# Seven products in place of eight for pairs of token blocks, in a retention and feed-forward kernel on one core

## The chip, the core and the metric

The program runs on one core of a Trainium2 chip. The metric is the time of one execution on the device in microseconds (us); lower is better. The engines have names of their own: PE (TensorE) multiplies matrices into PSUM, ACT (ScalarE) and DVE (VectorE) do elementwise work, POOL (GpSimd) does elementwise work on SBUF, and SP (SyncE) issues nearly all DMA transfers. Each engine takes its instructions strictly in the order of the program.

## The reference

```
scores = q @ k.T / sqrt(64)                      # 8 batches, 8 heads, 576 positions, head size 64
D[h,i,j] = gamma_h ** (i - j) if i >= j else 0   # gamma_h = 1 - 2**(-5-h)
x = (scores * D) @ v                             # 4608 tokens x 512
h = x @ w_in                                     # 512 -> 2048: the first product
out = (h - tanh(h)) @ w_out                      # 2048 -> 512: the second product
```

All arrays are float32.

## The kernel before

The 576 positions are cut into NC = 9 blocks of C = 64. A block holds 64 positions of all 8 batches, so BLK = 512 tokens. Per block three things are done.

*Retention* (`entry`, `entry3`; the matmuls have L287): for each batch and head 64x64 matmuls give the scores within the block (`s`), the new state (`new`) and the output (`own`, `two`), which adds the running `state` of the earlier blocks. The output x is written as two fp32r words, `xh` (rounded) and `xl` (the rest). From the third block on, a block's retention is three calls of `entry3` that lie in the FFN work of the block before. Its q, k and v are loaded by SP (`qk`, `vr`, `one`) and scaled by tables on POOL (`prep`, L237).

*First product* (`mm1`, L430): for each of NF = 16 slices f of the 2048 hidden columns, 12 matmuls of 128x128 weights by 512 tokens gather h(n, f) in one PSUM bank: 4 slices of the 512 inputs, times the three terms w_high·x_high, w_high·x_low, w_low·x_high. The bank is one of two (tag `h`).

*Second product* (`mm2`, L495): ACT makes tanh (L455), DVE subtracts (L456), ACT rounds `gh` (L457), DVE makes the rest `gl` (L458); then 12 matmuls of 512 columns add this slice into the four banks `o0` to `o3`. After slice 15 the banks are copied to `ob` and stored.

The weights arrive as raw words and are turned into two fp32r words each (`win`, `wout`), which stay in SBUF from then on. While this goes on, blocks 0 and 1 only do their first product (`seq`); its results go to DRAM (`spill`) and come back later in the loop `late`, which does the second products of block 1 and then of block 0 (`fetch`, `resume`, `words`). Blocks 2 to 8 then alternate `mm1` of one slice with `mm2` of the slice before. `in_order` holds each engine to the order in which the code is written. Tiles share places by `tag`; `bufs` is how many of a tag exist, and a tile that takes a place waits until all readers of the last one there are done.

## Time and profile before

| | |
|---|---|
| median of 3 runs | 882.23 us (882.13 to 883.61) |
| span of the profiled execution, first to last instruction | 881.9 us |
| time of that execution beside the span | none is listed; the median is 0.3 us above the span |
| PE busy | 872.7 us |
| DVE, ACT, POOL busy | 367.3, 294.4, 69.4 us |
| DMA | 82.06 MB, mean 93 GB/s |

A row of groups names the line, the engine, the operation, output <- inputs with their shapes, the count, and then busy us, mean ns of one, and idle time before. Matmuls overlap in the pipeline, so a matmul's duration in a row is longer than its share of the time; the chain of waits gives start, length and count of stretches of them. "PEclk" is the share of TensorE's clock that was granted.

### The profile page before, as it was taken

The page shows a single profiled execution, that of the slowest core. Times are in us where ns is not written, and L with a number is a line of the kernel's source. Part 1 is how long each engine was busy: PE and PEld are TensorE (multiplying, and loading weights), DVE is VectorE, ACT ScalarE, POOL GpSimd, SP SyncE. Part 2 cuts the span into 40 slices and gives each one's busy share as a digit, 9 for nine tenths or more (in the row PEclk, how much of TensorE's full clock was granted, in tenths as well). Part 3 has the DMA queues.
Part 4 walks back from the last instruction along what each step waited for, and adds up shares of the span by engine and source line. Part 5 has one row for each costly group of instructions (what it writes and reads, how often), then busy time and mean ns, then how long its engine had stood idle before and what let it go on. Part 6 is the DMA issues. An engine that isn't in the chain of part 4 may idle for free.

```text
span 881.9 us, 17730 instructions
## 1 busy us (share of the span) xinstructions
PE 872.7 (99%) x7846; PEld 724.3 (82%) x7846; DVE 367.3 (42%) x571; ACT 294.4 (33%) x525; POOL 69.4 (8%) x73
## 2 busy tenths in 40 slices
PE   7999999999999999999999999999999999999997
PEld 6888888888888888888888888888888888888886
DVE  5989876554332333323332433233232332232222
ACT  4887754443222222222222222222222222222222
POOL 0001001011110001101110111001110111000000
PEclk9999999999999999999999999999999999999999
DMA  8966945552410121203220141112120321002001
GB/s 307 374 237 220 367 154 167 142 164 77 116 49 30 49 68 55 78 1 97 73 79 1 50 119 50 30 47 62 62 78 1 97 73 48 1 2 48 1 1 48
DMA packets 37628, 82.06 MB, mean 93 GB/s; under 512 B 4144, under 2 KB 5296, under 8 KB 37552
## 3 DMA queue, kind: packets, MB, share of 16 engines
q1 hardware_dynamic: 37024, 80.02, 28.5%
q8 instruction: 61, 1.00, 0.5%
q10 hardware_dynamic: 528, 0.92, 0.3%
q14 instruction: 15, 0.12, 0.0%
HBM read 63.62 MB, written 17.30 MB: 92 GB/s over the span
## 4 chain that ended last, share of the span: by engine, by line
PE 98%; DMA 1%; ACT 0%; DVE 0%; SPq 0%; issue 0%
PE o L495 45%; PE h L430 45%; PE new L287 2%; PE s L287 2%; PE own L287 2%; PE two L287 1%; DMA rwi<-in_w_in_dram 1%; DMA a<-in_first_dram 1%; PE new_first L287 0%; PE own_first L287 0%; SPq L555 0%; ACT mi L100 0%; ACT xh L313 0%; ACT mi L105 0%; PE s_first L287 0%
## 5 line engine op out<-in xcount | busy, mean ns | idle before, releaser
L430 PE MATMUL h<-xh,wi 128*128 128x512 f32 x1152 | 302.8, 391 | 0.5 <-ACT xh L313 0.5
L495 PE MATMUL o<-wo,gh 128*128 128x512 f32 x1144 | 289.8, 391 | 0.0
L430 PEld LDWEIGHTS h<-xh,wi 128*128 128x128 f32 x1152 | 216.3, 188 | 46.3 <-ACT xh L313 0.7
L495 PEld LDWEIGHTS o<-wo,gh 128*128 128x128 f32 x1144 | 213.1, 188 | 45.0
L456 DVE TENSOR_TENSOR g<-h,g 128x512 f32<-128x512 f32 x114 | 78.8, 691 | 341.5 <-ACT g L455 341.4
L455 ACT ACTIVATE g<-h 128x512 f32<-128x512 f32 x114 | 68.2, 598 | 363.6 <-PE h L430 362.8
L495 PE MATMUL o<-wo,gl 128*128 128x512 f32 x572 | 157.2, 389 | 0.0
L430 PE MATMUL h<-xl,wi 128*128 128x512 f32 x576 | 154.2, 389 | 0.0
L430 PEld LDWEIGHTS h<-xl,wi 128*128 128x128 f32 x576 | 108.1, 188 | 22.6
L495 PEld LDWEIGHTS o<-wo,gl 128*128 128x128 f32 x572 | 107.4, 188 | 22.3
L458 DVE TENSOR_TENSOR gl<-g,gh 128x512 fp32r<-128x512 f32 x113 | 81.0, 717 | 77.6 <-ACT gh L457 72.8
L457 ACT CAST gh<-g 128x512 fp32r<-128x512 f32 x113 | 70.1, 621 | 86.0 <-DVE g L456 86.0
L237 POOL TENSOR_TENSOR vr<-vr,vtab 128x512 f32<-128x512 f32 x21 | 22.4, 1068 | 611.0 <-DMA vr<-in_qkv_dram 525.3
L287 PE MATMUL own<-qk,state 64*64 64x64 f32 x736 | 45.2, 221 | 0.0
L287 PE MATMUL own<-qk,vr 64*64 64x64 f32 x736 | 44.1, 218 | 0.0
L287 PEld LDWEIGHTS own<-qk,vr 64*64 64x64 f32 x736 | 36.8, 135 | 0.0
L287 PEld LDWEIGHTS own<-qk,state 64*64 64x64 f32 x736 | 36.7, 134 | 0.0
L478 DVE TENSOR_TENSOR gl<-s,gh 128x512 fp32r<-128x512 f32 x30 | 23.1, 770 | 24.2 <-PE o L495 13.6
L237 POOL TENSOR_TENSOR qk<-qk,qtab 128x512 f32<-128x512 f32 x20 | 28.4, 1421 | 53.5 <-DMA qk<-in_qkv_dram 53.5
L477 ACT CAST gh<-s 128x512 fp32r<-128x512 f32 x30 | 18.6, 621 | 30.0 <-PE o L495 17.3
L287 PE MATMUL s<-qk 64*64 64x64 f32 x736 | 25.5, 219 | 0.0
L313 ACT CAST xh<-own 128x512 fp32r<-128x512 f32 x25 | 14.7, 586 | 29.9 <-PE own L287 29.9
(85 smaller groups left out, 568.6 us busy)
## 6 DMA issues: line engine op xcount, KB each, us to landing
qk<-in_qkv_dram SPq DMA_DIRECT2D x23, 512.0 KB, 5.9
vr<-in_qkv_dram SPq DMA_DIRECT2D x23, 512.0 KB, 4.5
rwi<-in_w_in_dram SPq DMA_DIRECT2D x16, 512.0 KB, 5.4
rwo<-in_w_out_dram SPq DMA_DIRECT2D x16, 512.0 KB, 5.2
out_dram<-ob SPq DMA_DIRECT2D x61, 128.0 KB, 2.4
s<-spill_dram SPq DMA_DIRECT2D x30, 256.0 KB, 2.7
one<-in_qkv_dram SPq DMA_DIRECT2D x14, 512.0 KB, 5.4
spill_dram<-g SPq DMA_DIRECT2D x20, 256.0 KB, 4.3
```

The lines of the kernel that those rows point to most:

```text
L237: nc.gpsimd.tensor_tensor(a, a, table, op=ALU.mult)
L287: nc.tensor.matmul(out_, w, x, start=start, stop=stop)
L313: nc.scalar.copy(xh, o)
L430: nc.tensor.matmul(hp, win[f][:, a, cc, :], x[:, cc, :], start=(k == 0), stop=(k == 3 * NCC - 1))
L455: nc.scalar.activation(g, h, AF.Tanh)
L456: nc.vector.tensor_tensor(g, h, g, op=ALU.subtract)
L457: nc.scalar.copy(gh, g)
L458: nc.vector.tensor_tensor(gl, g, gh.bitcast(F32), op=ALU.subtract)
L477: nc.scalar.copy(gh, g)
L478: nc.vector.tensor_tensor(gl, g, gh.bitcast(F32), op=ALU.subtract)
L495: nc.tensor.matmul(ops[n][t], g[:, t * P : (t + 1) * P], wout[f_][:, a, :], start=(f_ == first and k == 0), stop=(f_ == final and k == 2),)
```

## The change

For blocks 3 to 8, taken in pairs (3,4), (5,6), (7,8), the first product is done for two blocks and two slices f at once. Tokens (block a, block b), inputs (two halves) and hidden columns (slice 2j, slice 2j+1) form 2x2 matrices of blocks, and the Winograd form of Strassen's scheme makes their product from seven products instead of eight, each with half the inputs: 2 slices times 3 terms = 6 matmuls of 512 columns (`product`).

- *Variants of the weights.* For each of 8 pairs of slices seven 256x128 weight matrices are needed. Three are pieces of the weights themselves, which `raw_words` writes to DRAM (`wvar`) during the second half of `late`. Four are sums (`variants`: POOL makes `r1`, `r2`, half of `ta` and of `tb`, DVE the other halves; ACT rounds, DVE makes the rest into `ot`, SP stores). They are made while block 2 does its first product.
- *Block 2* now does its whole first product at once; h - tanh(h) goes to DRAM, and its second product follows as a stage of its own (`stage_b(2, 0)`).
- *Stage A* (`stage_a`) of a pair does seven products for each j, additions on DVE, and block a's second product (`mm2_pair`). Block b's h - tanh(h) goes to DRAM. The variants come back from DRAM in slots of four (`load_slot`, 1 MB).
- *Stage B* (`stage_b`) is block b's second product alone, and between its slices the retention of the next pair: eight calls of `attend`, two batches each, for block a and block b in turn. It also makes the seven sums of tokens (`put`): hi words on ACT, low words on DVE, `t1`, `t3` on DVE and `t2`, `t4` on POOL.
- The loads of q, k, v and their scaling on POOL now go by turns of two batches (`load_turn`, `prep_turn`).

The core of the diff (`split`, `mm2_pair`, the new tags and the removed code of blocks 2 to 8 in other places are left out):

```diff
+NV = 7
+NPAIR = NF // 2
+FIRST = 3
...
-        if n == 0 or n == 1 and f < NF - 2:
+        if n == 1 and f >= NF - 2:
+            activate(n, f, hp, g)
+        elif n < 2:
 
             nc.scalar.copy(g, hp)
             pace.append(tc.nc.cur_bb.bb.instructions[-1].name)
             nc.sync.dma_start(spill[n, f], g)
         else:
-            activate(n, f, hp, g)
-
...
+            nc.scalar.activation(g, hp, AF.Tanh)
+            nc.vector.tensor_tensor(g, hp, g, op=ALU.subtract)
+            nc.sync.dma_start(spill[n, f], g)
...
+    def raw_words(f):
+
+        j, w = f // 2, win[f].bitcast(F32)
+        for v, cc in ((0, 0), (5, 2)) if f % 2 == 0 else ((6, 2),):
+            nc.sync.dma_start(wvar[:, NV * j + v].rearrange("p (s m) -> p s m", s=2), w[:, :, cc : cc + 2].rearrange("p s c m -> p s (c m)"))
+
...
+    turns = [(c + u) * B + b for c in range(FIRST, NC, 2) for b in range(0, B, 2) for u in range(2)]
+    work = pool.tile([P, 4, DM], F32, tag="xl1", bufs=1, name="work")
...
+    def load_turn(m, t):
+        if m >= len(turns):
+            return
+        j = turns[m]
+        c, b = divmod(j, B)
+        if t == 0 and (m == 1 or m % 8 == 0):
+            load_tables(c - m % 2)
+        if t == 0 and m % 3 == 2:
+            part = const.tile([P, 2, 2, 4, C], F32, tag=place_of(0), name=f"qk{j}")
+        elif t == 0:
+            part = pool.tile([P, 2, 2, 4, C], F32, tag="qk", bufs=2, name=f"qk{j}")
+        else:
+            part = pool.tile([P, 2, 2, 4, C], F32, tag=("vr", "one")[m % 2], bufs=1, name=f"vr{j}")
+        nc.sync.dma_start(part, qkv_d[c - 1, b : b + 2, :, 2 * t : 2 * t + 2].rearrange("u p t i s -> p u t i s"))
+        parts[j, t] = part
+        for u in range(2):
+            loaded.setdefault(j + u, Parts([None, None])).parts[t] = part[:, u]
...
+    def put(v, b, src, sub):
+
+        hi, lo = [x[:, :, b * C : (b + 2) * C].rearrange("p i (u t) -> p u i t", u=2) for x in xv[v]]
+        if sub == 0:
+            nc.scalar.copy(hi, src)
+        else:
+            nc.vector.tensor_tensor(lo, src, hi.bitcast(F32), op=ALU.subtract)
...
+    def attend(m, between):
+
+        j = turns[m]
+        c, b = divmod(j, B)
+        first, states = (c - FIRST) % 2 == 0, c < NC - 1
+        if first and b == 0:
+            new_xv()
+        o = bank(f"own{j}", "own")
+        outs, same = pair(m_out, j, o), []
+        if states:
+            new = bank(f"new{j}", "new")
+            same += pair(m_state, j, new)
+        more = m + 1 < len(turns)
+        if more:
+            sc = bank(f"s{turns[m + 1]}", "h")
+            same = pair(m_score, turns[m + 1], sc) + same
+        run(same, outs)
+        if more:
+            after_score(turns[m + 1], sc, 2)
+        if first:
+            a = pool.tile([P, 2, 4, C], F32, tag="cv", bufs=4, name=f"xa{j}")
+            kept[b] = a
+            put(0, b, o[:, :, 0:2], 0)
+            put(5, b, o[:, :, 2:4], 0)
+            nc.scalar.copy(a, o)
+            if states:
+                add_state(j, new)
+            between()
+            put(0, b, o[:, :, 0:2], 1)
+            put(5, b, o[:, :, 2:4], 1)
+        else:
+            a = kept.pop(b)
+            t13 = pool.tile([P, 2, 2, 2, C], F32, tag="cv", bufs=4, name=f"t13_{j}")
+            t24 = pool.tile([P, 2, 2, 2, C], F32, tag="cv", bufs=4, name=f"t24_{j}")
+            t1, t3, t2, t4 = t13[:, 0], t13[:, 1], t24[:, 0], t24[:, 1]
+            own = pool.tile([P, 2, 4, C], F32, tag="cv", bufs=4, name=f"xb{j}")
+            nc.scalar.copy(own, o)
+            put(4, b, o[:, :, 2:4], 0)
+            nc.vector.tensor_tensor(t3, own[:, :, 2:4], own[:, :, 0:2], op=ALU.subtract)
+            nc.gpsimd.tensor_tensor(t2, t3, a[:, :, 0:2], op=ALU.add)
+            nc.vector.tensor_tensor(t1, own[:, :, 0:2], a[:, :, 0:2], op=ALU.subtract)
+            nc.gpsimd.tensor_tensor(t4, a[:, :, 2:4], t2, op=ALU.subtract)
+            if states:
+                add_state(j, new)
+            put(3, b, t3, 0)
+            put(2, b, t1, 0)
+            between()
+            put(4, b, o[:, :, 2:4], 1)
+            put(3, b, t3, 1)
+            put(2, b, t1, 1)
+            put(1, b, t2, 0)
+            put(6, b, t4, 0)
+            put(1, b, t2, 1)
+            put(6, b, t4, 1)
+        prep_turn(m + 2, 0)
+        prep_turn(m + 1, 1)
+        load_turn(m + 3, 0)
+        load_turn(m + 2, 1)
...
+    def variants(j):
+
+        f1, f2 = [win[2 * j + u].bitcast(F32) for u in range(2)]
+        r1, r2, ta, tb = [pool.tile([P, 2, 2, P], F32, tag="cv", bufs=4, name=f"{n}{j}") for n in ("r1", "r2", "ta", "tb")]
+        if j == 0:
+            ots = [pool.tile([P, 2, 2, 2, P], F32R, tag="xh1", bufs=1, name=f"ot{j}_{u}") for u in range(2)]
+        else:
+            ots = [const.tile([P, 2, 2, 2, P], F32R, tag=place_of(2 * j - 2 + u), name=f"ot{j}_{u}") for u in range(2)]
+        for r, f in ((r1, f1), (r2, f2)):
+            nc.gpsimd.tensor_tensor(
+                r.rearrange("p k c m -> p (k c) m"), f[:, 0], f[:, 1], op=ALU.add,
+            )
+        nc.gpsimd.tensor_tensor(ta[:, 1], r2[:, 0], r2[:, 1], op=ALU.add)
+        nc.gpsimd.tensor_tensor(tb[:, 0], r1[:, 0], r2[:, 0], op=ALU.subtract)
+        nc.vector.tensor_tensor(ta[:, 0], ta[:, 1], r1[:, 0], op=ALU.subtract)
+        nc.vector.tensor_tensor(tb[:, 1], r1[:, 1], ta[:, 0], op=ALU.subtract)
+        for u, t in enumerate((ta, tb)):
+            nc.scalar.copy(ots[u][:, :, 0], t)
+            nc.vector.tensor_tensor(ots[u][:, :, 1], t, ots[u][:, :, 0].bitcast(F32), op=ALU.subtract)
+            nc.sync.dma_start(
+                wvar[:, NV * j + 1 + 2 * u : NV * j + 3 + 2 * u], ots[u].bitcast(F32).rearrange("p v s c m -> p v (s c m)"),
+            )
...
+    def load_slot(n):
+
+        if n >= per * ((NC - FIRST) // 2):
+            return
+        w = pool.tile([P, 4, 2, 2, P], F32R, tag=("xh0", "xh1", "xl0")[n % 3], bufs=1, name=f"ws{n}")
+        at = 4 * (n % per)
+        nc.sync.dma_start(w.bitcast(F32).rearrange("p v s c m -> p v (s c m)"), wvar[:, at : at + 4])
+        slots[n] = w
+
+    count = [0]
+
+    def product(v, into, start=True):
+
+        n, at = divmod(count[0], 4)
+        w, (xh, xl) = slots[n][:, at], xv[v]
+        terms = [(a, x, k) for a, x in ((0, xh), (0, xl), (1, xh)) for k in range(2)]
+        for i, (a, x, k) in enumerate(terms):
+            nc.tensor.matmul(
+                into, w[:, a, k], x[:, k], start=start and i == 0, stop=i == len(terms) - 1, skip_group_check=not start,
+            )
+        count[0] += 1
+        if at == 3:
+            load_slot(n + 3)
...
+    def stage_a(na):
+
+        nb = na + 1
+        u2, u4 = work[:, 0], work[:, 1]
+        for j in range(NPAIR):
+            x, y = [psp.tile([P, BLK], F32, tag=t, bufs=1, name=f"p{t}{na}_{j}") for t in ("new", "own")]
+            z, v = [psp.tile([P, BLK], F32, tag="h", bufs=2, name=f"p{t}{na}_{j}") for t in "zv"]
+            f1, f2 = 2 * j, 2 * j + 1
+            c22, c12, c21 = [pool.tile([P, BLK], F32, tag="g", bufs=3, name=f"c{t}_{na}_{j}") for t in (22, 12, 21)]
+
+            def tanh(c):
+                th = pool.tile([P, BLK], F32, tag="cv", bufs=4, name=f"th{na}_{j}")
+                nc.scalar.activation(th, c, AF.Tanh)
+                return th
+
+            def away(c, f):
+                nc.gpsimd.tensor_tensor(c, c, tanh(c), op=ALU.subtract)
+                nc.sync.dma_start(spill[nb, f], c)
+
+            product(0, x)
+            product(1, y)
+            nc.scalar.copy(u2, x)
+            nc.vector.tensor_tensor(u2, y, u2, op=ALU.add)
+            product(2, z)
+            nc.vector.tensor_tensor(u4, z, u2, op=ALU.add)
+            product(3, v)
+            nc.vector.tensor_tensor(c22, v, u4, op=ALU.add)
+            y = psp.tile([P, BLK], F32, tag="own", bufs=1, name=f"py{na}_{j}")
+            product(4, y)
+            away(c22, f2)
+            nc.vector.tensor_tensor(c12, y, u4, op=ALU.add)
+            product(5, x, False)
+            away(c12, f1)
+            g11 = tanh(x)
+            nc.vector.tensor_tensor(g11, x, g11, op=ALU.subtract)
+            product(6, v, False)
+            split(na, f1, g11, False)
+            nc.vector.tensor_tensor(c21, v, u2, op=ALU.add)
+            nc.vector.tensor_tensor(c21, c21, tanh(c21), op=ALU.subtract)
+            if j > 0:
+                mm2_pair(na, j - 1)
+            split(na, f2, c21, True)
+        for f in range(3):
+            fetch(nb, f)
+        mm2_pair(na, NPAIR - 1)
+        for f in range(2):
+            split(nb, f, fetched.pop((nb, f)), False)
+
+    def stage_b(n, m0):
+
         for f in range(NF):
-            mm1(n, f)
-            todo.append((n, f))
-            if len(todo) > 1 and (n, f) != (NC - 1, NF - 2):
-                mm2(*todo.pop(0))
-            if n + 1 < NC and f in (2, 6, 14):
-
-                entry3((n + 1) * B + (0, 2, 5)[(2, 6, 14).index(f)])
-                mm2(*todo.pop(0))
-    mm2(NC - 1, NF - 1)
+            def ahead():
+                if f + 3 < NF:
+                    fetch(n, f + 3)
+                if f + 2 < NF:
+                    split(n, f + 2, fetched.pop((n, f + 2)), f % 3 == 0)
+
+            if f % 2 == 0 and n < NC - 1:
+                attend(m0 + f // 2, ahead)
+            else:
+                ahead()
+            if (n, f) != (NC - 1, NF - 2):
+                mm2(n, f)
+
+
+    for f in range(NF):
+        mm1(2, f)
+        if f == 0:
+            mm2(*late[-1])
+        if f % 2 == 1:
+            variants(f // 2)
+        if f == 8:
+            load_turn(1, 0)
+            load_turn(2, 0)
+            load_turn(1, 1)
+        if f == 11:
+            prep_turn(1, 0)
+    for f in range(3):
+        fetch(2, f)
+    for n in range(3):
+        load_slot(n)
+    for f in range(2):
+        split(2, f, fetched.pop((2, f)), False)
+    stage_b(2, 0)
+    for s in range((NC - FIRST) // 2):
+        stage_a(FIRST + 2 * s)
+        stage_b(FIRST + 2 * s + 1, 8 * (s + 1))
```

How the order moves, at three places. ACT, block 2's first product, from the tanh of slice 1 on (`g_1` is slice 1; `ot_0`, `ot_1` are the rounded sums of one pair j, `xh` the retention of block 3). Before:

```order
L455 ACTIVATE g_1_2658<-h_1_2645 128x512
L457 CAST gh_1_2659<-g_1_2658 128x512
L455 ACTIVATE g_2_2694<-h_2_2681 128x512
L457 CAST gh_2_2695<-g_2_2694 128x512
L313 CAST xh_2781<-own_2713 128x2x4x64
```

Now:

```order
L451 ACTIVATE g_1_2677<-h_1_2664 128x512
L843 CAST ot_0_2685<-ta_2683 128x2x256
L843 CAST ot_1_2686<-tb_2684 128x2x256
L451 ACTIVATE g_2_2712<-h_2_2699 128x512
L451 ACTIVATE g_3_2729<-h_3_2716 128x512
```

The rounding of `gh` has left this place, and two roundings of `ot` stand ahead of the tanh of slice 2. For j = 0 both `ot` tiles have the one place of tag `xh1`.

SP, from the end of block 2's first product to the start of its second (`spill_dram<-g` writes slice 13, 14, 15; `s` brings a slice back; `ws` is a slot of variants). Before, the same place, after block 0's stores:

```order
L517 DMA out_dram<-ob_3_2641 64x512 x2
L209 DMA vr_2786<-in_qkv_dram 128x2x512
L223 DMA one_2789<-in_qkv_dram 128x1024
L209 DMA qk_2793<-in_qkv_dram 128x2x512
L209 DMA vr_3035<-in_qkv_dram 128x2x512
```

Now:

```order
L453 DMA spill_dram<-g_14_3032 128x512
L453 DMA spill_dram<-g_15_3049 128x512
L845 DMA wvar_dram<-ot_0_3057 128x1024
L845 DMA wvar_dram<-ot_1_3058 128x1024
L459 DMA s_0_3071<-spill_dram 128x512
L459 DMA s_1_3073<-spill_dram 128x512
L459 DMA s_2_3075<-spill_dram 128x512
L858 DMA ws_3077<-wvar_dram 128x2048
L858 DMA ws_3079<-wvar_dram 128x2048
L858 DMA ws_3081<-wvar_dram 128x2048
L459 DMA s_3_3178<-spill_dram 128x512
```

Before, only inputs of the retention are loaded here; now the fetch of block 2's first slice stands behind the stores of the last variants.

POOL, retention under block 2's FFN work (`t_32` are the tiles of t1 to t4; `qk` and `vr` are scaled in place). Before:

```order
L237 TENSOR_TENSOR vr_2786<-vr_2786,vtab 128x2x256
L237 TENSOR_TENSOR one_2789<-one_2789,vtab 128x256
L237 TENSOR_TENSOR one_2789<-one_2789,qtab_2262 128x256
L237 TENSOR_TENSOR qk_2793<-qk_2793,qtab_2262 128x2x256
L237 TENSOR_TENSOR vr_3035<-vr_3035,vtab 128x2x256
```

Now:

```order
L805 TENSOR_TENSOR t_32_3294<-t_32_3293,xa_3173 128x256
L807 TENSOR_TENSOR t_32_3294<-xa_3173,t_32_3294 128x256
L240 TENSOR_TENSOR qk_3187<-qk_3187,work 128x2x256
L240 TENSOR_TENSOR vr_3189<-vr_3189,vtab 128x2x256
L240 TENSOR_TENSOR qk_3320<-qk_3320,work 128x2x256
L240 TENSOR_TENSOR vr_3322<-vr_3322,vtab 128x2x256
```

In every second call of `attend` the two sums t2, t4 now stand ahead of the scaling for the next calls.

More of the change, by code (lines that the diff above doesn't have):

```diff
@@ L68, in retention_ffn @@
 @with_exitstack
-def retention_ffn(ctx: ExitStack, tc: tile.TileContext, ins, out, spill):
+def retention_ffn(ctx: ExitStack, tc: tile.TileContext, ins, out, spill, wvar):
     nc = tc.nc
@@ L344, in entry, with entry3 @@
         add_state(j, new)
-    def entry3(j, later=None):
+    def entry3(j, later):
         c0, b = divmod(j, B)
@@ new lines, in retention_ffn, with place_of, load_tables @@
+    work = pool.tile([P, 4, DM], F32, tag="xl1", bufs=1, name="work")
+    def place_of(f):
+        return place("i", f) if f != 1 else "wi14"
+    def load_tables(c):
+        both = work[:, 2].rearrange("p (n i s) -> p n i s", n=2, i=4)
+        nc.sync.dma_start(both, qtab_d[c - 1 : c + 1].rearrange("n p i s -> p n i s"))
+        for u in range(2):
+            qtabs[c + u] = both[:, u]
+    def load_turn(m, t):
[13 more added lines that the diff above has]
+        parts[j, t] = part
+        for u in range(2):
+            loaded.setdefault(j + u, Parts([None, None])).parts[t] = part[:, u]
@@ new lines, in retention_ffn @@
+    slots = {}
+    per = NV * NPAIR // 4
+    def load_slot(n):
[17 more added lines that the diff above has]
+            load_slot(n + 3)
```

84 lines of the change are left out of this document (56 added, 28 removed).

## The prediction, made before the change was run

> **What bounds the kernel now.** I read the page's busy times and its chain first.
>
> ```profile
> span 881.9 us, 17730 instructions
> PE 872.7 (99%) x7846; PEld 724.3 (82%) x7846; DVE 367.3 (42%) x571; ACT 294.4 (33%) x525; POOL 69.4 (8%) x73
> PE 98%; DMA 1%; ACT 0%; DVE 0%; SPq 0%; issue 0%
> ```
>
> PE is the bound nearly everywhere, so a matmul that goes is worth its full time. What it is worth stands in the chain in order of time (start, length, what):
>
> ```profile
> 590.71 2.95 PE o L495 x12
> 593.65 5.44 PE h L430 x24
> ...
> 686.37 2.95 PE o L495 x12
> ```
>
> 24 matmuls take 5.44 us, 0.2267 each. From 590.71 to 686.37 is one block, 95.66 us: 384 matmuls (87.0) and three entries of retention (8.6, or 2.9 each). The 12 matmuls behind an entry take 2.95, not 2.72: 0.23 for the hand-over. The other engines in that block, and in the later half of the loop `late` (busy us per engine, granted clock, DMA share, GB/s):
>
> ```profile
> 590.00:686.00 96.00, 96.00 (x933) 79.91 (x928) 31.78 (x50) 24.06 (x42) 10.60 (x10) 1.00 0.20 57
> 170.00:210.00 40.00, 40.00 (x356) 33.29 (x355) 22.89 (x36) 17.54 (x31) 3.65 (x4) 1.00 0.51 154
> ```
>
> DVE, ACT and POOL (third to fifth) are a third busy or less. But the new work is bunched and chained, so I price it link by link, with these groups (busy, mean ns):
>
> ```profile
> L237 POOL TENSOR_TENSOR one<-one,qtab 128x256 f32<-128x256 f32 x14 | 10.3, 739 | 0.0
> L237 POOL TENSOR_TENSOR vr<-vr,vtab 128x512 f32<-128x512 f32 x21 | 22.4, 1068 | 611.0 <-DMA vr<-in_qkv_dram 525.3 <-ACT mi L105 66.5 <-PE o L495 19.2
> L456 DVE TENSOR_TENSOR g<-h,g 128x512 f32<-128x512 f32 x114 | 78.8, 691 | 341.5 <-ACT g L455 341.4
> L299 DVE TENSOR_TENSOR one<-two,mask 128x256 f32<-128x256 f32 x14 | 5.9, 424 | 10.4 <-PE two L287 10.4
> L457 ACT CAST gh<-g 128x512 fp32r<-128x512 f32 x113 | 70.1, 621 | 86.0 <-DVE g L456 86.0
> ```
>
> and these transfers (KB each, median us to landing); the row in SP's timeline is its issuing of one:
>
> ```profile
> out_dram<-ob SPq DMA_DIRECT2D x2, 512.0 KB, 5.6
> spill_dram<-g SPq DMA_DIRECT2D x20, 256.0 KB, 4.3
> s<-spill_dram SPq DMA_DIRECT2D x30, 256.0 KB, 2.7
> out_dram<-ob SPq DMA_DIRECT2D x61, 128.0 KB, 2.4
> qk<-in_qkv_dram SPq DMA_DIRECT2D x23, 512.0 KB, 5.9
> 0.74 0.39 SPq L555 DMA_DIRECT2D a<-in_first_dram  x1
> ```
>
> Two more things decide. **POOL and DVE exclude each other** when DVE has both inputs in SBUF. In the timeline (start, length):
>
> ```profile
> 309.44 1.29 POOL L237 TENSOR_TENSOR qk<-qk,qtab 128x512 f32<-128x512 f32 x1 [1.11 <-DMA qk<-in_qkv_dram]
> 310.04 0.69 DVE L456 TENSOR_TENSOR g<-h,g 128x512 f32<-128x512 f32 x1 [4.60 <-ACT g L455]
> 526.54 1.29 POOL L237 TENSOR_TENSOR qk<-qk,qtab 128x512 f32<-128x512 f32 x1
> 526.77 1.61 DVE L458 TENSOR_TENSOR gl<-g,gh 128x512 fp32r<-128x512 f32 x1 [0.69 <-ACT gh L457]
> 622.43 0.69 DVE L458 TENSOR_TENSOR gl<-g,gh 128x512 fp32r<-128x512 f32 x1 [0.69 <-ACT gh L457]
> 622.43 1.84 POOL L237 TENSOR_TENSOR qk<-qk,qtab 128x512 f32<-128x512 f32 x1
> ```
>
> With an input in PSUM (310.04) both keep their times. `gl` (526.77) waits until POOL ends at 527.83 and is done 0.55 later; at 622.43 DVE is first and POOL's 1.29 becomes 1.84.
>
> **PE's clock falls after a gap** (us, busy, and PEclk ahead of the last two columns):
>
> ```profile
> 13.00:14.00 1.00, 0.49 (x24) 0.35 (x24) 0.70 (x3) 0.62 (x1) 0.00 (x0) 1.00 0.72 190
> 14.00:15.00 1.00, 0.32 (x8) 0.21 (x8) 0.00 (x0) 0.00 (x0) 0.00 (x0) 1.00 0.92 368
> 15.00:16.00 1.00, 0.64 (x40) 0.65 (x38) 0.83 (x2) 0.37 (x1) 0.00 (x0) 1.00 1.06 418
> 16.00:17.00 1.00, 0.93 (x33) 0.79 (x26) 0.87 (x3) 0.74 (x2) 0.00 (x0) 0.92 1.01 401
> 17.00:18.00 1.00, 0.57 (x12) 0.38 (x8) 0.89 (x2) 0.39 (x2) 0.00 (x0) 0.50 0.91 270
> 18.00:19.00 1.00, 0.97 (x2) 0.83 (x3) 0.64 (x2) 0.97 (x3) 0.00 (x0) 0.50 0.97 327
> 19.00:20.00 1.00, 1.00 (x4) 0.75 (x3) 0.93 (x3) 0.97 (x3) 0.00 (x0) 0.50 1.01 362
> 20.00:21.00 1.00, 1.00 (x5) 0.80 (x4) 0.93 (x4) 0.95 (x3) 0.00 (x0) 0.87 0.95 351
> ```
>
> After three half-idle us the clock lacks 0.08+0.5+0.5+0.5+0.13 = 1.7 us of work.
>
> **The change, part by part.**
>
> *Removed:* per pair of blocks 384 matmuls become 8x7x6 = 336; three pairs save 144 x 0.2267 = **-32.6**.
>
> *Retention by fours:* the matmuls stay, one hand-over per block is added: 6 x 0.23 = **+1.4** (from 0 to 6 x 2.9).
>
> *First variants (hole 1).* Count from the start of block 2's first product: slice 0 to 2.7, block 0's last second product to 5.4, slices 1, 2, 3 to 13.6. Slice 4 needs the bank of slice 2, so DVE's subtract of slice 2, which is queued behind variants(0). Those start late: POOL's outputs take `cv` places that hold block 0's `ob`. SP issues a spill and eight stores at 0.4 from 4.1 on, and the `ob` tiles are free at 7.3 to 10.1 (2.4 to land); POOL's 1.29+1.29+0.74+0.74 end at 11.3, DVE's two halves at 12.1, ACT's rounding and DVE's low word at 14.0, the last held up by POOL's next sum. Now `ot_1` needs the place of `ot_0`, so ACT stops until that 512 KB store lands: 4.3 to 5.9 by the rows, 5.2 taken, nearer the 512 KB rows; 19.2. Behind ACT's wait stand the tanh of slices 2 and 3, behind DVE's the subtracts. Rounding 0.6, low word 0.7, subtract 0.7: slice 4 starts at 21.2 instead of 13.6, **+7.6** (5 to 8.5).
>
> *The other variants.* Per pair of slices PE needs 5.44 us. POOL's four sums are 4.1, DVE's four operations on SBUF 2.2 (2 x 0.42 + 2 x 0.69); excluded from each other, less 0.14 for each that waited, they take 5.7, and with the hand-overs (DVE's halves wait for POOL's `ta`, POOL's next `r1` for DVE's `tb`) and the next subtract behind them I get 6.2. After hole 1 there is a lead; five pairs lose 0.7: **+3.6** (0 to 8).
>
> *To block 2's second product (hole 2).* From the end of slice 15: subtract 1.5; DVE's halves and low words are slowed by POOL's two scalings (1.3+1.1) that stand there, so the last `ot` store is issued at 6.9 (3.9 without them), and SP can issue the fetch of slice 0 only then. It lands behind 1 MB of stores and 0.6 later `gh` is there: 10.2 (7.6 without exclusion or queue). PE has one attend, 2.2. **+8.0** (5 to 10). What is late next: the fetch of slice 3 stands behind three slots of 1 MB, some 10 us, and just makes it.
>
> *Clock:* both holes are longer than the gaps in the rows: 2 x 1.7 = **+3.4** (0 to 5).
>
> *Odd attends.* POOL starts t2 when ACT's copy and DVE's t3 are done, 1.1 after the attend; t2, t4, then the scalings `qk` and `vr`, with a DVE operation let in between each: 0.3 + 0.74 + 0.74 + 0.55 + 1.29 + 0.28 + 1.04, so `vr` is ready at 6.1. The next attend starts 5.4 after the last and needs `vr` with its third matmul. 0.7 for each of the three odd calls per stage that another call follows, nine: **+6.3** (0 to 9; without exclusion it is ready at 4.9 and costs nothing).
>
> *Costed at nothing.* Stage A: per j PE has 66 matmuls, 15.0 us, against 9 DVE operations (6.2), 7 of ACT (4.3), POOL 2.6, and 2.4 MB of DMA (158 GB/s). A slot is needed at least 10.9 us after its place is free, and 16.3 except at a stage's start; 1 MB takes 3.5 at 302 GB/s (154 / 0.51, the window of `late`). If that cover goes, each late slot costs its excess. The raw words: below. Stage B's fetches come 7 us ahead.
>
> Sum: -32.6 + 1.4 + 7.6 + 3.6 + 8.0 + 3.4 + 6.3 = **-2.3**. Against the span of 881.9 that is 879.6; the median stands 0.3 above the span, so **880**. 0.2% (1.8 us) is about what a measurement here can tell from no change; the forecast lies just beyond it.
>
> The Trainium skill, "SBUF — State Buffer", section "Who interferes with whom", states the exclusion as a rule: a Vector instruction with two SBUF inputs contends with a GpSimd instruction that reads SBUF, and the one that comes second is blocked for the whole of the other. The six rows agree (1.61 and 1.84). It speaks against this change: by it the sum is as above, and without it some 870.
>
> **The rivals.**
>
> *A: POOL and DVE rarely meet.* The exclusion is seen at a handful of places, and a shift of 0.5 us undoes the odd attends. Then +3.6 and +6.3 go: 870.
>
> *B, slower: the raw words choke the second half of `late`.* 24 stores of 256 KB, 6.3 MB, in 16 steps of 2.72 us are 145 GB/s; the window leaves 0.49 x 302 = 148. They are cut into 1 KB pieces, half the spill's. If a byte costs twice there, the backlog is (290 - 148) / 302 x 43.5 = 20 us; the fetches go out four steps (10.9 us) ahead, so PE stands some 9.5: 890. It decides from 1.5 times the cost per byte on. For it: nothing in the rows is as finely cut at this rate. Against: just that.
>
> The Trainium skill, "DMA: Bandwidth & Descriptors", section "Specifications", has pieces of 512 B and more at full rate; by that B does not happen and 880 stands. No row here shows 1 KB pieces.
>
> *C: the holes are small.* If the stores land in 2.4 and the clock stays up, holes of 5 and 5 and no exclusion leave 882.2 - 32.6 + 1.4 + 10 = 861. Against it, every transfer of 256 KB or more takes longer.
>
> **How the numbers follow.** Forecast 0.50, with its own range 874 to 887 from the bounds of its terms taken together; A 0.22, B 0.20, C 0.08. Of the forecast's half, 0.19 is faster by over 0.2%, 0.17 within, 0.14 slower. Faster 0.19 + 0.22 + 0.08 = 0.49, same 0.17, slower 0.34. The range 866 to 892 leaves out C and the outer part of B and A.
>
> **What would show it.** Hole 1: in the waits, ACT's `ot` on a DMA for about 5 us, PE's `h` on DVE for 7 to 8. Hole 2: PE's `o` waiting for ACT's `gh` about 8 us after one attend. PEclk at 0.5 after both. POOL as releaser of `own` in nine attends. Stage A with PE gapless, about 115 us. It is wrong if PE waits for a slot in stage A, or if `late` itself gets longer.

## The result, and the profile after

The changed kernel takes 887.3 us, median of four runs (886.6 to 891.5), against 882.9 (882.1 to 883.6) for the kernel before: ratio 1.0063, 95% interval 1.0040 to 1.0086. It is slower by some 5 us. The prediction said 880.0, 2.2 us faster than before. The measured time lies within its range of 866 to 892, but the kernel became slower and not faster.

The page of the changed kernel: span, busy times, shares of the chain, transfers, and the granted clock in 40 slices of 22 us.

```profile
span 884.8 us, 18546 instructions
PE 851.0 (96%) x7701; PEld 699.6 (79%) x7702; DVE 491.2 (56%) x742; ACT 340.6 (38%) x633; POOL 188.2 (21%) x165
PE 84%; DMA 7%; DVE 4%; ACT 2%; issue 2%; POOL 0%; SPq 0%; ACTq 0%; DVEq 0%; POOLq 0%
DMA packets 72580, 174.54 MB, mean 197 GB/s; under 512 B 7472, under 2 KB 14896, under 8 KB 67120
PEclk9999999999897999999999999999999999999999
```

PE's busy time fell from 872.7 to 851.0 us, but PE now holds 84% of the chain and not 98%: it is made to wait. The bytes moved have more than doubled, from 82 to 175 MB. Where PE waits (us in total, times, longest):

```profile
PE h L434 <- DVE g L452: 7.8, 4, 5.4
PE o L489 <- ACT gh L884: 7.6, 1, 7.6
PE own L290 <- DVE xlv L762: 3.1, 3, 1.4
PE s L290 <- POOL ta L838: 0.9, 1, 0.9
```

The same by stage: block 2's first product, block 2's second product with the retention of blocks 3 and 4, then stage A and stage B of the first two pairs (us, busy per engine, granted clock, DMA share, GB/s):

```profile
213.30:272.10 58.80, 49.94 (x209) 39.01 (x208) 36.72 (x46) 18.32 (x32) 35.70 (x33) 0.94 0.63 223
272.10:349.40 77.30, 65.43 (x1217) 53.89 (x1218) 46.83 (x72) 25.06 (x56) 27.27 (x25) 0.93 0.70 241
349.40:469.60 120.20, 120.09 (x533) 98.86 (x531) 51.90 (x77) 36.42 (x61) 23.40 (x18) 1.00 0.53 176
469.60:532.90 63.30, 62.34 (x1217) 51.91 (x1217) 44.64 (x68) 23.22 (x53) 24.98 (x22) 1.00 0.64 203
532.90:653.10 120.20, 120.09 (x529) 98.83 (x527) 51.93 (x77) 36.38 (x61) 23.41 (x18) 1.00 0.53 176
653.10:716.10 63.00, 61.98 (x1057) 51.63 (x1057) 42.11 (x65) 23.19 (x53) 21.26 (x19) 1.00 0.50 159
```

Stage A is the gain: 120.2 us for 528 matmuls at 0.2267, which is 119.7, with no gap over 0.3 us. The loss is in the first two rows. The first product's 204 matmuls are 46.2 us and it takes 58.8. The second product takes 77.3, and the same work with eight calls of `attend` takes 63.3 one pair later. These 26.6 us are most of what stands against the 32.6 us of removed matmuls. A later pair (120.2 and 63.0) takes 183.2 us where two blocks took 191.3 before, so each pair by itself gains 8 us.

The two holes in windows of 5 us (PE's busy time is the first number behind the length, the clock stands third from the end):

```profile
225.00:230.00 5.00, 2.07 (x10) 1.38 (x8) 2.68 (x2) 0.62 (x1) 4.47 (x4) 0.94 0.26 108
230.00:235.00 5.00, 2.57 (x6) 2.09 (x7) 3.65 (x6) 2.35 (x5) 2.25 (x3) 0.50 0.47 186
235.00:240.00 5.00, 5.00 (x20) 4.04 (x20) 2.88 (x3) 1.01 (x3) 4.08 (x4) 0.87 0.58 233
...
260.00:265.00 5.00, 2.91 (x14) 2.09 (x12) 3.38 (x3) 0.60 (x1) 4.92 (x5) 1.00 1.02 400
270.00:275.00 5.00, 3.25 (x134) 2.59 (x132) 4.96 (x7) 1.84 (x4) 4.31 (x5) 1.00 0.69 270
275.00:280.00 5.00, 0.00 (x0) 0.00 (x0) 1.39 (x2) 0.05 (x1) 0.24 (x1) 0.72 0.80 283
280.00:285.00 5.00, 3.28 (x8) 2.60 (x9) 3.30 (x6) 2.79 (x6) 0.00 (x0) 0.50 0.92 307
285.00:290.00 5.00, 5.00 (x18) 3.75 (x16) 0.52 (x2) 0.00 (x0) 0.00 (x0) 0.75 1.02 427
```

PE stands about 226.9 to 232.4 and 274 to 281.7, and in and after each hole half the clock is granted. Between them, at 260 to 265, is a third, smaller one, in which the transfers are full (share 1.02). ACT's timeline (start, us, and in brackets what it waited for) names all three:

```profile
230.44 0.62 ACT L843 CAST ot<-tb 128x512 fp32r<-128x512 f32 x1 [4.79 <-DMA wvar_dram<-ot]
263.60 0.60 ACT L451 ACTIVATE g<-h 128x512 f32<-128x512 f32 x1 [3.79 <-DMA spill_dram<-g]
281.05 1.28 ACT L884 CAST gh<-s 128x512 fp32r<-128x512 f32 x2 [6.00 <-DMA s<-spill_dram]
```

The first is the store of `ot_0`, whose place `ot_1` needs. The second is a tanh that needs a place of tag `g`, which a spill still holds. The third is the fetch of slice 0, which SP issued at 276.91, behind the last store of `ot` at 275.82:

```profile
275.82 1.00 SPq L845 DMA_DIRECT2D wvar_dram<-ot  x2
276.91 2.30 SPq L459 DMA_DIRECT2D s<-spill_dram  x3
279.30 1.36 SPq L858 DMA_DIRECT2D ws<-wvar_dram  x3
```

### The profile page after: what moved, and what is told of

It is laid out like the page before. It is cut to its first block, busy times and chain, and to the rows that moved or that the text cites. A ratio compares the mean times of both kernels' runs of the same rounds, so it can differ in the third digit from the quotient of the medians.

```text
span 884.8 us, 18546 instructions
## 1 busy us (share of the span) xinstructions
PE 851.0 (96%) x7701; PEld 699.6 (79%) x7702; DVE 491.2 (56%) x742; ACT 340.6 (38%) x633; POOL 188.2 (21%) x165
## 4 chain that ended last, share of the span: by engine, by line
PE 84%; DMA 7%; DVE 4%; ACT 2%; issue 2%; POOL 0%; SPq 0%; ACTq 0%; DVEq 0%; POOLq 0%
PE o L489 25%; PE o L900 15%; PE h L434 12%; PE pnew L869 7%; PE pv L869 7%; PE pown L869 4%; PE py L869 4%; PE pz L869 4%; DMA s<-spill_dram 3%; PE own L290 3%; PE s L290 3%; PE new L290 2%; DMA spill_dram<-g 1%; DVE ot L844 1%; DMA qk<-in_qkv_dram 1%
## 5 line engine op out<-in xcount | busy, mean ns | idle before, releaser
L489 PE MATMUL o<-wo,gh 128*128 128x512 f32 x608 | 158.2, 398 | 8.5 <-ACT gh L884 7.6
L489 PEld LDWEIGHTS o<-wo,gh 128*128 128x128 f32 x608 | 113.8, 190 | 34.6 <-ACT gh L884 8.0
L923 POOL TENSOR_TENSOR c<-c,th 128x512 f32<-128x512 f32 x48 | 62.1, 1296 | 269.1 <-ACT th L919 267.9
L434 PE MATMUL h<-xh,wi 128*128 128x512 f32 x384 | 100.3, 397 | 9.0 <-DVE g L452 7.8
L434 PEld LDWEIGHTS h<-xh,wi 128*128 128x128 f32 x384 | 71.6, 190 | 27.4 <-DVE g L452 10.4
L489 PE MATMUL o<-wo,gl 128*128 128x512 f32 x304 | 85.0, 392 | 0.0
L900 PE MATMUL o<-wo,gs 128*128 128x512 f32 x288 | 70.6, 389 | 0.0
L900 PEld LDWEIGHTS o<-wo,gs 128*128 128x128 f32 x288 | 54.1, 188 | 11.2
L869 PE MATMUL pnew<-xhv,ws 128*128 128x512 f32 x192 | 59.5, 391 | 0.3
L489 PE MATMUL o<-wo,gs 128*128 128x512 f32 x240 | 59.2, 394 | 0.0
L434 PE MATMUL h<-xl,wi 128*128 128x512 f32 x192 | 52.4, 395 | 0.0
L489 PEld LDWEIGHTS o<-wo,gs 128*128 128x128 f32 x240 | 44.3, 188 | 9.6
L900 PE MATMUL o<-wo,gh 128*128 128x512 f32 x192 | 48.9, 389 | 0.0
```

Source lines behind the costliest of these rows:

```text
L434: nc.tensor.matmul(hp, win[f][:, a, cc, :], x[:, cc, :], start=(k == 0), stop=(k == 3 * NCC - 1))
L489: nc.tensor.matmul(ops[n][t], g[:, t * P : (t + 1) * P], wout[f_][:, a, :], start=(f_ == first and k == 0), stop=(f_ == final and k == 2),)
L869: nc.tensor.matmul(into, w[:, a, k], x[:, k], start=start and i == 0, stop=i == len(terms) - 1, skip_group_check=not start,)
L900: nc.tensor.matmul(ops[n][t], g[:, t * P : (t + 1) * P], wout[f][:, a, :], start=(j == 0 and f == fs[0] and k == 0), stop=last_,)
L923: nc.gpsimd.tensor_tensor(c, c, tanh(c), op=ALU.subtract)
```

## The experiments

Each kernel was timed beside the kernel before, which stood at 882.8 to 883.3 us in these runs; ratios are to it, with 95% intervals. To compare with the changed kernel, subtract 1.0063, whose own interval is 0.0046 wide: with a run's own interval, a difference of less than some 2.5 us is not told apart. The kernels with the change also scatter more (run 9 from 872.5 to 883.7, the kernel before beside it from 882.3 to 884.6), and a profiled execution is one of these: run 3's was 4.8 us above its median, run 5's 2.6 below. One source of the scatter is seen. In the stage B at 469, whose code these kernels share, PE waits for `own` on `xlv` 0.3 us in the profile of the change, and 1.9, 2.1 and 2.1 in those of runs 1, 3 and 7. So a trace below shows which wait went, and the median what it was worth.

| | median us | ratio |
|---|---|---|
| the change | 887.3 | 1.0063 (1.0040 to 1.0086) |
| 1: two places for `ot` | 886.2 | 1.0040 (1.0023 to 1.0058) |
| 2: fetch first | 893.3 | 1.0116 (1.0098 to 1.0134) |
| 3: no sums | 875.3 | 0.9924 (0.9896 to 0.9952) |
| 4: clock kept | 884.8 | 1.0021 (1.0007 to 1.0036) |
| 5: low words first | 884.2 | 1.0011 (0.9998 to 1.0024) |
| 6: scaling first | 883.7 | 1.0000 (0.9987 to 1.0013) |
| 7: two slices kept | 887.0 | 1.0038 (1.0023 to 1.0053) |
| 8: kept, and places | 883.8 | 1.0005 (0.9991 to 1.0019) |
| 9: 8 and slots later | 880.3 | 0.9962 (0.9944 to 0.9980) |
| 10: 8 with 5 and 6 | 876.8 | 0.9928 (0.9916 to 0.9940) |
| 11: 8 with 5, 6 and slots later | 872.0 | 0.9873 (0.9857 to 0.9890) |
| 12: 11 and loads spread | 870.0 | 0.9858 (0.9835 to 0.9882) |

**1. Two places for `ot`.**

```diff
-            ots = [pool.tile([P, 2, 2, 2, P], F32R, tag="xh1", bufs=1, name=f"ot{j}_{u}") for u in range(2)]
+            pair_ = pool.tile([P, 2, 2, 2, 2, P], F32R, tag="xh1", bufs=1, name="ot0")
+            ots = [pair_[:, u] for u in range(2)]
```

> Undoes one thing: the two rounded sums of the first pair of slices get a place each (both halves of one tile), so ACT does not wait for the first one's store. In the trace of the changed kernel PE stands 5.5 us there and the clock is at half for 3.8 us more of work (1.9). Theory (the shared place makes hole 1): PE's wait at slice 4 is gone and the time falls by 5 to 8 us against the changed kernel, 6.5 taken, since some of the lead is given back at the following pairs. Rival (the chain POOL, DVE, ACT of the sums is late anyway, and the store's wait only lies beside it): it falls by less than 2.5 us, and PE waits at the slices 4 and 6 for DVE.

The ratio falls by 0.0023, some 2 us: the rival's end, and too little to be told from nothing. In the trace PE's wait in hole 1 fell from 5.4 to 3.0 us, not to nothing:

```profile
PE h L434 <- DVE g L452: 4.4, 4, 3.0
```

The wait for the store was the last of two. Behind it stands the lateness of the sums, and it remains. Their wait for `cv` places, held by block 0's `ob`, is an estimated 1.5 us of it at most: DVE is done with slice 1's subtract at 223.28 and takes `ta` at 224.77. The rest is the length of the chain POOL, DVE, ACT itself. The prediction had both waits, and counted the lateness only as the start of the store's.

**2. The fetch of block 2's first slices ahead of the last variants.**

```diff
+        if f == NF - 1:
+            for g_ in range(2):
+                fetch(2, g_)
+            for g_ in range(2):
+                split(2, g_, fetched.pop((2, g_)), False)
         if f % 2 == 1:
             variants(f // 2)
...
-    for f in range(3):
-        fetch(2, f)
+    fetch(2, 2)
...
-    for f in range(2):
-        split(2, f, fetched.pop((2, f)), False)
```

> Moves one thing: the fetch and split of block 2's slices 0 and 1 are issued ahead of the last pair's sums and their stores, slice 2 behind them. Theory (SP's order makes hole 2): PE's wait behind the first attend falls from 7.7 to about 3.5 us and less of it is followed by half clock (2.9 now): 5 to 8 us less than the changed kernel, 6 taken. Rival (the transfers themselves are the limit: slice 0 can't come back faster in that traffic): less than 2.5 us.

Slower by some 5 us than the change. The hole fell from 7.6 to 5.0 us, but the last variants now stand behind two splits that wait for the fetch, their store is late, and the attends behind it wait (`own`, 3.6 us once):

```profile
PE o L489 <- ACT gh L884: 5.4, 2, 5.0
PE own L290 <- DVE xlv L762: 5.5, 3, 3.6
```

**3. No sums.** `variants` only stores raw words of the same size in the same places; the four sums of weights, their roundings and low words are left out, so the output is another.

```diff
-        (all of variants but the stores)
+        for u in range(2):
+            nc.sync.dma_start(
+                wvar[:, NV * j + 1 + 2 * u : NV * j + 3 + 2 * u], win[2 * j + u].bitcast(F32).rearrange("p s c m -> p (s c m)").rearrange("p (v m) -> p v m", v=2),
+            )
```

> Leaves out the sums of the weights: raw words of the same size are stored in their places, so DMA traffic and all later work stay. Theory (making the sums costs both holes and the slow slices of block 2): hole 1 with its clock (7.8), the POOL and DVE waits at the slices (about 1.8) and half of hole 2 with its clock (5) go: 12 to 17 us less than the changed kernel, 14 taken; the wait of ACT for a spill at slice 11 (2.3) stays. Rival (the stores and loads, not the sums, are what block 2's stage waits for): 3 to 7 us less.

Some 12 us less than the change. Block 2's first product took 48.4 us instead of 58.8, with one wait of 1.3 left for a spill. Hole 2 stayed:

```profile
PE o L489 <- ACT gh L868: 7.1, 1, 7.1
PE h L434 <- DVE g L452: 1.3, 1, 1.3
```

So hole 1 is the sums', with the clock lost after it, and hole 2 is not: SP still comes to the fetch (266.54) after spills and stores.

**4. The clock kept.** 22 idle matmuls (5.0 us) where hole 1 stands and 32 (7.3 us) where hole 2 stands, into a bank that holds nothing then.

```diff
+    def fill(n):
+        d = psp.tile([P, DM], F32, tag="o3", bufs=1, name=f"fill{n}")
+        for _ in range(n):
+            nc.tensor.matmul(d, wout[0][:, 0, :P], wout[0][:, 1, :], start=True, stop=True)
...
+        if f == 4:
+            fill(22)
         mm1(2, f)
...
                 attend(m0 + f // 2, ahead)
+                if (n, f) == (2, 0):
+                    fill(32)
```

> Adds matmuls whose result is not used: 22 of 512 columns ahead of slice 4 of block 2's first product and 32 behind the first attend, 5.0 and 7.3 us, so that PE is busy in most of both holes; the waits stay. Theory (a gap costs again as half clock behind it, 1.9 and 2.9 us): 3 to 5 us less than the changed kernel, 4.5 taken, PEclk at 1.00 there. Rival (the slow matmuls behind the holes hide other waits, or the fillers take as long as they save): within 1 us of the changed kernel.

As expected: the ratio falls by 0.0042, 3.7 us. The clock is 1.00 from 225 to 240 and from 270 to 290, and the page's row shows 9 throughout. A slice of that row is 22 us, though, and hides short falls: the clock still stands at 0.50 for 3.4 us at 264.9 and at 292.2, behind other waits.

```profile
PEclk9999999999999999999999999999999999999999
```

The holes cost 13.2 us of standing still, and a good quarter more in the slow clock behind them.

**5. Low words first.** In `attend`, DVE's `put`, which reads the bank `own`, ahead of `between()`, which splits a fetched slice.

```diff
-            between()
             put(0, b, o[:, :, 0:2], 1)
             put(5, b, o[:, :, 2:4], 1)
+            between()
...
-            between()
             put(4, b, o[:, :, 2:4], 1)
+            between()
```

> In each attend, the subtraction that makes the low words out of the PSUM bank own now stands ahead of the split of a fetched slice in VectorE's order, no longer behind it. Theory: the stalls of 3.1 us (own released by VectorE's xlv) and part of the ones that follow are due to that subtraction standing behind a split whose fetch is late; 3 to 5 us less than the changed kernel, about 883, and no wait of own on xlv in the list of waits. Rival: the split itself is then late for the second product, and the wait moves to o or s; within 1 us of the changed kernel.

The ratio falls by 0.0052, 4.6 us. What it cures is seen in the changed kernel's DVE timeline:

```profile
297.65 1.34 DVE L885 TENSOR_TENSOR gl<-s,gh 128x512 fp32r<-128x512 f32 x1 [2.27 <-ACT gh L884]
298.92 0.41 DVE L762 TENSOR_TENSOR xlv<-own,xhv 128x256 fp32r<-128x256 f32 x1
```

There is one bank `own`. The next attend may write it only when `xlv` has read it, `xlv` stands behind the low word of a slice, and that slice has just come. PE's next matmul into `own` starts at 299.47. In this run `own` on `xlv` is gone from the first rows of the list of waits.

**6. Scaling first.**

```diff
         if more:
             after_score(turns[m + 1], sc, 2)
+        prep_turn(m + 2, 0)
+        prep_turn(m + 1, 1)
...
-        prep_turn(m + 2, 0)
-        prep_turn(m + 1, 1)
         load_turn(m + 3, 0)
```

> In each attend, the scaling of a later attend's vr and the work beside it are issued right after the scores of this one, ahead of the sums of the variants and not behind them. Theory of the prediction's term of 0.7 us for each odd attend: GpSimd's sums push the scaling back; with the scaling ahead of them 1 to 3 us less than the changed kernel, 884 to 886. Rival: the sums are what is late, and each sum pushed back delays its store and the next load; 0 to 3 us more, 887 to 890.

The ratio falls by 0.0063, 5.6 us, more than was expected, but not for that reason. PE's waits for the scaled `vr` (`new` and `own`, put down to "issue") did not go in the profiled run. The changed kernel, then this run:

```profile
PE new L290 <- issue: 1.8, 2, 1.2
PE own L290 <- issue: 1.0, 1, 1.0
```

```profile
PE new L290 <- issue: 2.8, 2, 1.6
PE own L290 <- issue: 2.5, 1, 2.5
```

What fell is a wait of SP's in block 2's second product, for POOL's scaling by the old tables, whose place the load of the new ones needs. Again the changed kernel, then this run:

```profile
SPq L719 <- POOL qk L240: 9.4, 1, 9.4
```

```profile
SPq L719 <- POOL qk L240: 2.6, 1, 2.6
```

The fetches of two slices stand behind that load: SP issued it at 331.17 and them from 332.67 on, and at 323.44 and from 327.31 on in this run. The gaps of 1.6 and 0.4 us before the last attend of a stage, at 340 and 525, are gone. They are 2.0 us, and the profiled execution as a whole is only 0.5 us shorter than that of the change. So the trace shows which wait fell; where the rest of the 5.6 us comes from stays open.

**7. Two slices kept.** Slices 0 and 1 of block 2 are split straight from SBUF.

```diff
             nc.vector.tensor_tensor(g, hp, g, op=ALU.subtract)
-            nc.sync.dma_start(spill[n, f], g)
+            if f < 2:
+                split(n, f, g, False)
+            else:
+                nc.sync.dma_start(spill[n, f], g)
...
-    for f in range(3):
-        fetch(2, f)
+    fetch(2, 2)
...
-    for f in range(2):
-        split(2, f, fetched.pop((2, f)), False)
```

> Slices 0 and 1 of block 2 are split from SBUF straight after their first product, and kept there; they no longer go out to DRAM and back. Theory: the second hole (7.7 us, 0.4 us beside it, and some 2.9 us lost to the lower clock after it) is the way through DRAM of the first slice alone, and goes; 9 to 11 us less than the changed kernel, 876 to 878. Rival: slice 2, fetched in the same place, lands too late just as well, and 4 us or less are won: 883 or above.

The theory fell: hole 2 is gone from the list, and of its 8 us and the clock behind it some 2 are won (ratio down by 0.0025, within what can't be told apart). The waits have moved to the next slices:

```profile
PE own L290 <- DVE xlv L765: 6.9, 4, 3.0
PE o L492 <- ACT gh L887: 2.1, 1, 2.1
```

**8. Both holes.** As 7, with 1, and the four operands of the first sums in `work` and not in `cv`.

```diff
+            r1, r2, ta, tb = [work[:, i].rearrange("p (k c m) -> p k c m", k=2, c=2) for i in range(4)]
```

> Both holes: slices 0 and 1 of block 2 kept in SBUF as in the run before, and the variants of the first half get a place each for their sums and their four operands, so that neither a store of sums nor a store of the block before holds them. Theory: the first hole (5.5 us, and some 1.9 us lost to the lower clock after it) is a wait for places alone; with both gone 16 to 19 us less than the changed kernel, 868 to 871, which is faster than the kernel before by some 12. Rival: as in the run with two places, only part of the first hole goes (the operands' loads and the sums themselves take as long), and the sum is 873 to 877.

5 us less than the change, not 16 to 19, and level with the kernel before. Block 2's first product took 54.4 us, its second 75.5. Hole 1 did not go with the places. PE's waits, and DVE's timeline:

```profile
PE h L434 <- DVE g L452: 3.8, 4, 2.6
```

```profile
224.78 1.28 DVE L890 TENSOR_TENSOR gl<-g,gh 128x512 fp32r<-128x512 f32 x1 [0.69 <-ACT gh L889]
225.99 0.95 DVE L845 TENSOR_TENSOR work<-work 128x256 f32<-128x256 f32 x1
```

POOL's sums are done at 218.31, but DVE makes its halves only at 225.99, behind the low word of slice 1 that this run's split puts ahead of them. So what the places gave was partly taken back by the order on DVE. SP's and ACT's timelines show what held the second product:

```profile
273.67 0.48 SPq L462 DMA_DIRECT2D s<-spill_dram  x1
274.20 2.21 SPq L863 DMA_DIRECT2D ws<-wvar_dram  x3
276.45 0.44 SPq L462 DMA_DIRECT2D s<-spill_dram  x1
```

```profile
287.33 0.62 ACT L889 CAST gh<-s 128x512 fp32r<-128x512 f32 x1 [8.95 <-DMA s<-spill_dram]
```

Three slots of 1 MB, which stage A needs from 344 on, are loaded ahead of the fetch of slice 3, and ACT waits 8.95 us for a fetch.

**9. Slots later**, on top of 8.

```diff
+            if n == 2 and f in (4, 8, 12):
+                load_slot(f // 4 - 1)
...
-    for n in range(3):
-        load_slot(n)
```

> The run with both slices kept and with places of their own, and the first three loads of variants for the products of block 3 (1 MB each, not needed before some 344 us) issued after slices 4, 8 and 12 of block 2's second product, not ahead of the fetches of slices 3 and 4. Theory: what held those two runs near the kernel before is these 3 MB, which stand ahead of the fetches (the wait of 9.0 us of ScalarE for a fetch, with 3.3 and 3.2 us of TensorE behind it); 4 to 6 us less than that run, 878 to 880. Rival: the transfers are saturated by the stores and the operands of the attends anyway; within 1.5 us of it, 882 to 885.

The ratio falls by 0.0043 against 8, 3.8 us: a little under the theory's 4 to 6, and well over the rival's 1.5.

**10. Run 8 with the orders of 5 and 6.**

> The run with both slices kept and with places of their own, and in the attends the low words first and the scaling first, as in the two runs of those alone. Theory: the holes' successors and the hand-overs of the attends are apart, so the gains of about 3 us each (886.6 to 887.3 against 884.2 and 883.7) add: 4 to 6 us less than 883.8, 878 to 880. Rival: they come out of one and the same queue of late fetches; within 2 us of it, 882 to 884.

6.8 us less than 8 (0.0077), more than the theory's 4 to 6. By the table the two orders alone were worth 4.6 and 5.6, so their gains add only in part; in the traces, each of the two runs ends the gap at 340. The wait for the fetch that the slots hold up is then PE's own largest:

```profile
PE o L492 <- ACT gh L889: 5.4, 1, 5.4
```

**11. Run 10 with the slots later.**

> All of both: two slices kept, places, low words first, scaling first, and the three loads of variants later. Theory (late fetches behind the 3 MB on the one hand, order on VectorE and GpSimd on the other): 873 to 876. Rival (one common cause): 878 to 880, no more than the better of the two runs that it joins.

872.0: 4.9 us less than 10 and 7.9 less than 9, so these are two causes. By stage (the same columns as above):

```profile
214.40:267.30 52.90, 48.09 (x209) 37.66 (x207) 37.53 (x48) 19.37 (x34) 36.10 (x34) 1.00 0.66 238
267.30:332.20 64.90, 62.12 (x1217) 51.45 (x1218) 43.56 (x72) 24.53 (x54) 27.69 (x25) 1.00 0.81 278
332.20:452.40 120.20, 120.09 (x533) 98.83 (x531) 50.88 (x74) 36.38 (x61) 23.41 (x18) 1.00 0.53 177
```

Block 2's second product has fallen from 77.3 to 64.9 us, near the 62.9 of the next one, and the clock is whole. The first has 52.9 against 46.2.

**12. Run 11 with the loads of turns 1 and 2 spread.**

```diff
-        if f == 8:
-            load_turn(1, 0)
-            load_turn(2, 0)
-            load_turn(1, 1)
+        if f in (4, 8, 12):
+            load_turn(*{4: (1, 0), 8: (1, 1), 12: (2, 0)}[f])
```

> As the run with all of both, and the operands of turns 1 and 2 loaded at slices 4, 8 and 12 of block 2's first product, not all at slice 8. Theory: ScalarE's wait for a store of slice 8 to 9 (2.25 us of TensorE in the changed kernel, 1.0 in the run with both) comes from these 2 MB at once; 1 to 2 us less than the run with all of both. Rival: the stores of variants and slices fill the engines of the transfers anyway; no difference above 0.5 us.

870.0 against 872.0; the intervals overlap (0.9835 to 0.9882, 0.9857 to 0.9890), so this step alone isn't shown, and the profiled run still has a gap of 1.0 us at 259, as run 11 had. As a whole this kernel is 1.4% faster than the kernel before and 2.0% faster than the change.

## Why the prediction was wrong

From the start of block 2's first product to the last matmul, the trace of before has 663.5 us and that of the change 666.6. There are 144 matmuls fewer, 32.6 us, so 35.7 were lost where the prediction had 30.3. Matmul start by matmul start:

| term | predicted | measured |
|---|---|---|
| hand-overs and late attends | 1.4 + 6.3 | 9.3 |
| hole 1 | 7.6 | 5.9 |
| other variants (first product) | 3.6 | 4.0 |
| hole 2 | 8.0 | 8.1 |
| clock | 3.4 | 4.8 |
| the rest | 0 | 3.6 |

The 9.3 is the growth of the retention's time from 47.7 to 64.7 us less the 7.7 of hole 2, which stands inside it.

So the sign turned on 5.4 us: 3.6 of small gaps that the sum put at nothing, 1.6 of hand-overs and attends, 1.4 of clock, 0.5 of two other terms, less 1.7 of hole 1. The step of the mechanism that failed stands under "Costed at nothing": "Stage B's fetches come 7 us ahead." It counts SP as free, and SP was not. In the profile of the change, late fetches cost PE 3.1 us of waits for `own`, and the runs that change an order around them (5, 6, and 9 against 8) gain 4.6, 5.6 and 3.8 us.

- *Removed, 32.6:* right. In stage A no slot was late. "About 115 us" for it was a slip of arithmetic: 528 x 0.2267 is 119.7.
- *Hole 1:* the mechanism was right, ACT waits for the place of `ot`. What failed here is the 5.2 us taken for the store; it was issued at 227.73, landed 2.6 us later, and `ot_1` was rounded at 230.44. Run 1 showed that the late sums would have filled 3 of the 5.4 us anyway. The price of the sums as a whole (7.6 + 3.6 and 1.7 of clock, 12.9) is what run 3 measured, some 12.
- *The other variants:* 4.0 against 3.6, but by luck, for another reason. Waits of DVE's subtract took 0.7, a late POOL ahead of the first attend 1.1, and 2.25 was ACT's tanh at 263.60 waiting for a spill while the transfers were full. That the loads of q, k and v at slice 8 meet two kinds of stores there was not in the working. That they are the cause is not shown: run 12 spread them, and its gap of 1.0 us stayed.
- *Hole 2:* right in size, and in that the fetch stands behind the last store of `ot`. What it was worth was judged wrongly, as run 7 showed: hole 2 covers the lateness of the slices behind it. The prediction said of the fetch of slice 3 behind three slots that it "just makes it", and it was the next wait as soon as hole 2 went.
- *Clock:* mis-sized. 1.7 us per hole was taken from the start of the kernel; around hole 1 the clock stood at half for 6.8 us, 3.9 of them with work to do, and around hole 2 for 10.2, 5.7 with work, which lose 1.9 and 2.9. Run 4 got 3.7 of it back.
- *Odd attends:* the sum is 1.6 us short, the mechanism mostly wrong. POOL's late `vr` cost 1.3, 0.8 and 1.2 us, three times and not nine: 3.3 where the working had 6.3. As much, the 3.1 above, came from two things that the working did not have: the single bank `own` behind a split whose slice is late (run 5), and SP behind the load of tables, with the fetches behind it (run 6).
- *The rest:* 1.9 us in the stages from 349 on that hold no attend, in small gaps of up to 0.3; 1.1 more than before between the attends, one wait of 0.6 at 309 among them; 0.7 in block 2's first product. What causes them was not followed further.
- *The base:* the prediction set its sum against the span of 881.9 and put the median 0.3 above. Every listed run has 1.8 us between its time and its span, so that execution was the one of 883.6, the slowest of its three. The sum came to a span of 879.6 where 884.8 was measured, 5.2 off; the rest of the 6.6 us between a change of -2.2 and one of +4.4 is that slowest execution of before and a profiled execution of the change that was 0.7 below its median.

The rivals: B did not happen. `late` ends at 213.3 us in the change and at 213.5 before, so the raw words' stores in 1 KB pieces cost PE nothing. From 170 to 210 the DMA share is 0.87 at 280 GB/s, 322 for a full share, where before it was 0.51 at 154, 302: a byte cost no more than before. This agrees with the Trainium skill ("DMA: Bandwidth & Descriptors", section "Specifications"), which has pieces of 512 B and more at full rate. C did not happen: the holes were 5.9 and 8.1 us, and the clock fell. A was half right: of its 9.9 us, 5.1 (0.7, 1.1 and 3.3) are put down to POOL and DVE. The exclusion of the two is there in the change too. DVE's low word of a sum, 0.69 us alone, takes 1.77 when POOL adds beside it, and POOL's scaling, 1.29 alone, takes 1.75 in the odd attends. This agrees with the Trainium skill, "SBUF — State Buffer", section "Who interferes with whom". Two rows of the timelines:

```profile
225.93 1.77 DVE L844 TENSOR_TENSOR ot<-ta,ot 128x512 fp32r<-128x512 f32 x1
```

```profile
329.39 1.75 POOL L240 TENSOR_TENSOR qk<-qk,work 128x512 f32<-128x512 f32 x1
```

## What to carry to other kernels

A saving on the engine that bounds the kernel is kept only where the other engines keep up; here it was paid back in the 136 us in which block 2's two products were pulled apart to make room, more by queues in order than by a lack of throughput: runs 8 and 11 move the same 173.49 MB and make the same sums, and are 12 us apart. When one wait is removed, ask what it covered: the edit against hole 2 alone gained 2 us, those against both holes 5, and together with later slots and two orders inside `attend` they gained 17 (run 11). On a queue strictly in order, put what is needed next ahead of what is large, and read a place that others wait for (a bank, a table) before starting on what may be late.

## What the runs showed of the hardware

The clock fell some 2.5 and 3.2 us into the two gaps, and came back 3.9 and 5.7 us after work had begun again, so one gap's price (1.9 and 2.9 us of work) differs from another's. Idle matmuls in the gaps, 22 and 32 in run 4, kept it at 1.00 there. With stores and loads mixed the transfers were full (share 1.02) in two windows of 5 us, at 400 and 427 GB/s. In run 8 a fetch of 256 KB was issued at 276.45, with 3 MB of loads just ahead of it and the share at 1.00 from 276.4 to 287.4; ACT could go on only at 287.33, 10.9 us later, where the median from issue to landing of such a fetch is 2.7 in the kernel before.
